# A Mamba-2 block with a SwiGLU feed-forward: the inverse roots of its norm loaded in four pieces, and its hand-written order renewed

## The chip, the cores and the metric

The kernel runs on one core of a Trainium2 chip. Times are microseconds of device time of that core; a comparison takes the median of the runs. TensorE (PE) multiplies matrices, VectorE (DVE) and ScalarE (ACT) do elementwise work and empty PSUM, GpSimd (POOL) does a little, and SyncE (SP) issues nearly all transfers. Each of them works through its own queue of instructions in order and waits on semaphores for the others.

## The reference

Two stages follow each other. The first is a state-space recurrence for 4 sequences with 8 heads, 768 tokens, 32 values and 16 states per head, worked out in chunks:

```python
L = np.exp(cum[:, :, :, None] - cum[:, :, None, :]) * causal
M = np.einsum('bhin,bhjn->bhij', Cc, Bc) * L
y = np.einsum('bhij,bhjd->bhid', M, xc) + inter      # inter: C times the state, decayed
state = decay_full * state + sum(B x, decayed)
```

Its output, as 3072 tokens of 256 values, goes through a norm and a feed-forward with 1536 hidden values:

```python
rms = np.sqrt(np.mean(x * x, axis=-1, keepdims=True) + 1e-06)
xn = x / rms * rms_g
g, val = xn @ w_gate, xn @ w_val
out = (g / (1 + np.exp(-g)) * val) @ w_out
```

The weights and the gain of the norm arrive in 64-bit floating point.

## The kernel before

The tokens are taken in 6 blocks of 512. Values lie with the features on the partitions: y, the squares and the normed input xn are tiles of 128 partitions by 2 x 512 tokens. Block 0 is computed while the weights arrive and are converted to fp32 (`fetch` loads a piece, `pow`, `man` and `wt` convert it on ACT and DVE). From tile 3 of block 0 on, each product with a weight matrix uses a scheme with 7 products in place of 8.

Every step of the kernel has a name, and one long string of about 1,550 names, written out by hand, gives the order in which the steps are issued. A name such as `2:P.5.3` is block 2, step P, arguments 5 and 3; a number behind a slash names a PSUM slot. Each step puts its instructions and its DMAs on the queues of the engines that it uses, so the string fixes the order on every queue. The semaphores follow from the tiles. The steps that are spoken of below:

- `P.k.j` (`product_gv`, L909): product k of 7 for hidden tile j, into one of two PSUM tiles "gate" or "val". `take.k.j` (L915, ACT) copies a partial result p out. `C.c.j` (L921, DVE) adds up c. `silu` (L930, ACT) and `hid` (L934, DVE) make the hidden values h. In block 0, `gate.f` (L825), `early.f.s` (L835) and `norm.f` (L846) do the same for the first tiles without the scheme.
- `s`, `s3`, `s2`, `s4` (L965 to L975, DVE) make combinations of h. `O.k.j` (L999) is product k of 7 with w_out, `Otake` (L1015) and `Oadd` (L1023, L1026) add them up into ob, `out.a` (L1031) and `quarter` (L1036) store. `o.f` (L941) is w_out in block 0.
- `bc.p`, `x.p` (L121, L128) load B, C and x of a pair of chunks; `turn` (L505) transposes B and C on TensorE; `T` (L516) and `Tt` (L1107) copy the result out; `dT` (L530) loads decays dT from rowe in DRAM, and `Td` (L536) multiplies by them. `g`, `gg` (L562) are the products C times B, `L`, `L1` (L601, L607) multiply them by the decays L, `y` (L699) makes the output and starts the additions to the states of the next pairs (L627), `S` (L641, L651) the states. `spread` (L461), `sub`, `ex` prepare L. `yt` (L758 or L763) and `sq` (L747, L749) take y and its squares out of PSUM. `row`, `rowout`, `rowe` (L1074 to L1088) write rows of sums and decays to DRAM. `cw.j` (L879) combines weights.

The norm of blocks 1 to 5 goes through DRAM. `ms` (L777) sums the squares on TensorE: for each of 4 groups of 128 tokens it writes 32 partitions that all hold the same 128 sums. `rs` (L786, L787, ACT) takes the inverse root of this 128 x 128 tile and stores it in DRAM as roots, 4 groups x 32 equal copies x 128 tokens (L790, 64 KB). `rb` (`spread_roots`, L792 to L795) loads them as a tile r of 128 partitions by 512 tokens, 256 KB: each partition reads copy 0 of the 4 groups, 2 KB in all. `xn` (`norm_apply`, L802) multiplies y by the gain and by r, `tx` (L886) makes differences of xn, and then the P products of the next block can start.

Of the kernel before, what the change touches and what calls it, by code (L numbers as in the profile page):

```python
# [20 lines left out]
def kernel(  # L21
# [33 lines left out]
    nc = tc.nc  # L55

    P = 128
    NB, NH, S, D = x.shape
# [5 lines left out]
    T = NB * S  # L64
# [3 lines left out]
    NT = TB // P  # L68
# [104 lines left out]
    parts = {}  # L173
# [31 lines left out]
    warm = const.tile([P, 256], BF16, name="warm")  # L205
    gcol = const.tile([P, 2], FP32, name="gcol")
# [29 lines left out]
    mid = mids[:, 0]  # L236
# [555 lines left out]
    def spread_roots(blk):  # L792
        ps["r", blk] = r = nrm.tile([P, TB], FP32, tag="sq2", name="r", bufs=1)
        nc.sync.dma_start(out=r.rearrange("p (t m) -> p t m", t=NT),
                          in_=roots[blk][:, 0].partition_broadcast(P))  # L795
# [367 lines left out]
    def of_chunk(n, fn):  # L1163
# [28 lines left out]
        0:warm 0:a 0:set 0:bc.0 0:bc.1 0:x.0 0:x.1 0:ident 0:fetch.0 0:ones 0:zeros 0:fetch.1 0:mean  # L1192
        0:head 0:upto 0:never 0:after 0:mid 0:upto2 0:gcol 0:mids 0:ident16 0:whole16 0:idle.7
        0:mask.0.0/1 0:whole 0:hmask 0:tmask 0:part 0:part2 0:sel 0:mask.1.1/0 0:fetch.5 0:after2
        0:aT 0:la0 0:kinks 0:mask.0.1/2 0:log4.0.4 0:r.0 0:parts.0 0:eps 0:log 0:d 0:dx 0:c*2 0:cx
        0:log4.4.2 0:log4.6.2 0:scale.0 0:bc.2 0:turn.0.1 0:T.0.1 0:Tt.0.0.1 0:Tt.0.1.1 0:sums.0.1
        0:exp.0.1 0:turn.0.0 0:Tt.0.1.0 0:T.0.0 0:Tt.0.0.0 0:sums.0.0 0:exp.0.0 0:fetch.2 0:turn.1.1
        0:T.1.1 0:Tt.1.0.1 0:Tt.1.1.1 0:scale.1 0:cc 0:g.0.1/2 0:L.0.1 0:turn.1.0 0:Tt.1.1.0
        0:Tt.1.0.0 0:T.1.0 0:sums.1.1 0:exp.1.1 0:A.0 0:S.0 0:A.1 0:S.1 0:man.0 0:g.0.0/1 0:L.0.0
        0:pow.0 0:wt.0 0:man.5 0:pow.1 0:never16 0:last.1 0:Tl.1 0:mask.1.0/2 0:sums.1.0 0:exp.1.0  # L1200
        0:g.1.0/0 0:L.1.0 0:scale.2 0:last.0 0:Tl.0 0:fetch.4 0:fetch.3 0:x.4 0:middles 0:man.1
        0:g.1.1/1 0:L.1.1 0:fetch.6 0:fetch.7 0:pow.5 0:wt.5 0:y.0/2 0:sq.0 0:pow.3 0:row.1
        0:rowout.1 0:rowe.1 0:yt.0 0:ydone.0 0:fetch.12 0:y.1/0 0:r.1 0:row.0 0:man.2 0:fetch.9
        0:fetch.8 0:wt.1 0:early.0.0/1 0:parts.1 0:man.6 0:mask.3/2 0:sums.3 0:pow.2 0:wt.2 0:rowe.0
        0:rowout.0 0:dT.2 1:dT.0 0:sq.1 0:ms.0 0:yt.1 0:ydone.1 0:early.0.1 0:pow.6 0:wt.6
        0:fetch.13 0:man.3 0:exp.3 0:rs.0 0:man.7 0:wt.3 0:turn.2 0:pow.4 0:xn.0 0:mask.2/0 0:sums.2
        0:exp.2 0:early.1.0/2 0:early.1.1 0:man.4 0:wt.4 0:gate.2/0 0:x.2 0:norm.0 0:norm.1 0:T.2
        0:Tt.2.0 0:Tt.2.1 0:Td.2 0:dT.3 0:gg.2/1 1:table 0:silu.0 0:hid.0 0:gate.3/2 0:tx.0 0:man.8
        0:pow.7 0:wt.7 0:L1.2.3 0:L1.2.2 0:man.9 0:silu.2 0:hid.2 0:L.2.0 0:pow.9 0:wt.9 0:A.2 0:S.2
        0:pow.8 0:wt.8 0:silu.3 0:hid.3 0:fetch.11 0:man.11 0:pow.11 0:gate.4/0 0:silu.4 0:hid.4  # L1210
        0:bc.3 0:scale.3 0:fetch.10 0:pow.10 0:man.10 0:cw.3 0:gate.5/1 0:silu.5 0:hid.5 0:x.3
        0:y.2/2 0:pow.12 0:S.3 0:yt.2 0:sq.2 0:ydone.2 0:switch.0 0:P.1.3 0:take.1.3 0:wt.10 0:wt.11
        0:fetch.14 0:switch.1 0:P.2.3 0:man.12 0:turn.3 0:T.3 0:Tt.3.1 0:Tt.3.0 0:Td.3 0:bc.5
        0:P.6.3 0:take.6.3 0:man.13 0:x.5 0:pow.14 0:P.1.4 0:gg.3/2 0:L1.3.2 0:L.3.0 0:L1.3.3 0:bc.4
        0:scale.4 0:P.7.3 0:scale.5 0:y.3/2 0:silu.1 0:C.11.3 0:take.7.3 0:P.5.3 0:P.4.3 0:P.2.4
        0:wt.12 0:pow.13 1:dT.1 0:fetch.18 1:S.0 1:S.1 0:sq.3 0:yt.3 0:ydone.3 0:C.22.3 0:silug.22.3
        0:P.3.3 0:take.1.4 0:silug.21.3 0:ms.1 0:silug.11.3 0:tok 0:fetch.16 0:tokout 0:cw.4 0:P.6.4
        0:C.11.4 0:P.5.4 0:silug.11.4 0:take.6.4 0:P.7.4 1:turn.1 0:wt.13 0:take.7.4 0:C.12.3
        0:silug.12.3 0:P.2.5 0:pow.16 0:man.14 0:hidg.22.3 0:hidg.21.3 0:P.1.5 0:hidg.11.3 0:wt.14
        0:take.1.5 0:o.0/2 1:bc.1 0:hidg.12.3 0:C.22.4 0:P.3.4 0:silug.22.4 0:fetch.15 0:pow.15  # L1220
        0:cw.5 0:P.6.5 0:hid.1 0:o.1 0:C.11.5 0:take.6.5 0:silug.11.5 0:man.15 0:fetch.17 0:fetch.19
        0:P.4.4 0:spread.10 0:C.12.4 0:pow.17 0:silug.12.4 0:silug.21.4 0:wt.15 0:man.17 0:P.5.5
        0:P.7.5 0:take.7.5 0:man.16 0:wt.16 0:pow.18 0:o.2 0:o.3 0:o.4 0:o.5 0:hidg.11.5 0:P.4.5
        0:cw.1 0:C.22.5 0:silug.22.5 1:two.0 0:spread.9 0:exps 0:wt.17 0:spread.8 0:man.18 0:wt.18
        0:rs.1 1:turn.0 0:hidg.11.4 0:hidg.21.4 0:hidg.22.4 1:T.0 1:Tt.0.0 0:silug.21.5 0:hidg.12.4
        0:P.3.5 0:C.12.5 0:man.19 0:pow.19 0:wt.19 0:hidg.21.5 0:silug.12.5 0:hidg.12.5 0:spread.11
        0:sub.11 0:ex.11 0:table.0 0:sub.8 0:o.6 0:o.7 0:o.8 0:o.9 0:o.10 1:T.1 1:Tt.1.0 0:rb.1
        0:xn.1 1:P.1.1 1:take.1.1 1:P.1.0 1:take.1.0 1:P.2.1 1:P.2.0 0:tx.1 1:P.6.1 1:take.6.1
        0:ex.8 0:hidg.22.5 0:o.11 1:P.7.1 0:sub.9 0:ex.9 1:take.7.1 1:bc.0 0:cw.0 1:P.6.0 2:bc.1
        1:C.11.1 1:P.5.1 0:sub.10 0:ex.10 1:x.0 1:cw.2 1:P.4.1 1:take.6.0 1:P.7.0 2:spread.2  # L1230
        1:C.11.0 1:P.5.0 0:table.1 1:C.22.1 1:P.3.1 1:silu.21.1 1:hid.21.1 1:P.1.2 1:C.12.1
        1:silu.11.1 1:hid.11.1 1:silu.22.1 1:hid.22.1 1:take.7.0 1:C.22.0 1:P.4.0 1:take.1.2
        1:silu.11.0 1:hid.11.0 1:silu.21.0 1:hid.21.0 1:silu.12.1 1:hid.12.1 1:two.4 1:P.2.2 1:P.6.2
        1:take.6.2 1:silu.22.0 1:hid.22.0 1:P.1.3 1:take.1.3 1:P.3.0 1:C.12.0 1:s.1 1:P.7.2
        1:take.7.2 1:P.6.3 1:C.11.2 1:take.6.3 1:silu.11.2 1:two.2 1:P.2.3 1:C.11.3 1:P.4.2
        1:silu.21.2 1:P.5.2 1:C.22.2 1:silu.22.2 1:hid.11.2 1:hid.21.2 1:hid.22.2 1:P.7.3 1:take.7.3
        1:P.5.3 1:C.22.3 0:put.0 0:put.1 0:put.3 1:P.3.2 1:C.12.2 1:Tt.0.1 1:Td.0 1:s3.1 1:P.4.3
        1:silu.21.3 1:hid.21.3 1:silu.11.3 1:hid.11.3 1:silu.12.2 1:hid.12.2 1:P.1.4 1:take.1.4
        1:P.3.3 1:C.12.3 1:silu.12.3 1:hid.12.3 0:put.2 1:Tt.1.1 1:Td.1 1:scale2.1 1:silu.22.3
        1:hid.22.3 1:s.3 1:P.1.5 1:take.1.5 1:P.2.5 1:C.11.5 1:silu.12.0 1:hid.12.0 1:P.6.4  # L1240
        1:take.6.4 1:P.2.4 1:C.11.4 1:silu.11.5 1:hid.11.5 1:P.6.5 1:take.6.5 1:P.7.4 1:take.7.4 1:g
        1:L 1:L1.2 1:P.7.5 1:take.7.5 1:L1.3 1:P.5.4 1:C.22.4 1:P.4.4 1:silu.21.4 1:scale2.0 1:P.5.5
        1:C.22.5 1:silu.22.5 1:hid.22.5 1:silu.11.4 1:hid.11.4 1:hid.21.4 1:y.0 1:P.3.4 1:C.12.4
        2:S.0 1:P.4.5 1:silu.21.5 1:hid.21.5 1:s.2 1:P.3.5 1:C.12.5 1:silu.22.4 1:hid.22.4 1:s.0
        1:O.2.0 1:O.2.1 1:silu.12.4 1:hid.12.4 1:s.4 1:s3.4 1:O.1.0 1:O.1.1 1:silu.12.5 1:hid.12.5
        1:O.4.0 1:O.1.2 1:O.1.3 1:x.1 1:y.1 2:S.1 1:sq 1:spread.0 1:yt 1:O.1.4 1:O.1.5 1:Otake.1
        1:s.5 1:exps 1:spread.2 1:s3.3 2:dT.0 1:O.4.1 1:O.4.2 1:O.5.0 1:s2.0 1:O.5.1 1:s2.1 1:O.5.2
        1:s2.2 1:O.5.3 1:O.5.4 1:s2.4 1:s2.3 1:O.5.5 1:s2.5 1:s3.2 1:s3.0 1:sub.2 1:ms 1:rs 1:O.6.0
        1:s4.0 1:O.6.1 1:O.6.2 1:s4.1 1:O.6.3 1:O.6.4 1:O.6.5 1:Otake.6 1:s4.3 1:s4.4 2:turn.0 2:T.0
        2:Tt.0.1 1:rb 1:s4.5 1:s4.2 1:s3.5 2:dT.1 2:turn.1 2:T.1 2:Tt.1.0 2:Tt.1.1 2:Tt.0.0 2:Td.0  # L1250
        1:sub.0 1:ex.0 1:O.2.2 1:O.7.0 1:O.7.1 1:O.7.2 1:O.7.3 1:O.7.4 1:O.7.5 1:Otake.7 1:Oadd.22
        2:scale2.1 1:O.4.3 1:O.4.4 1:O.4.5 1:Oadd.21 1:O.2.3 1:O.2.4 1:O.2.5 1:O.3.0 1:O.3.1 1:xn
        2:P.1.1 2:take.1.1 2:P.1.0 2:take.1.0 1:tx 1:ex.2 1:spread.1 1:sub.1 1:ex.1 1:O.3.2 1:O.3.3
        1:O.3.4 1:O.3.5 1:Oadd.12 1:spread.3 1:sub.3 1:ex.3 2:P.6.0 2:take.6.0 2:x.0 2:P.6.1
        2:take.6.1 1:Oadd.11 2:P.2.1 2:C.11.1 2:silu.11.1 2:P.2.0 2:C.11.0 2:silu.11.0 2:hid.11.0
        2:P.7.0 2:take.7.0 2:P.7.1 2:take.7.1 2:P.5.0 2:C.22.0 2:silu.22.0 2:P.5.1 2:C.22.1
        2:silu.22.1 2:P.4.0 2:silu.21.0 2:hid.21.0 2:P.4.1 2:silu.21.1 2:hid.21.1 2:hid.11.1 2:P.3.1
        2:C.12.1 2:silu.12.1 2:P.3.0 2:C.12.0 2:silu.12.0 2:hid.12.0 2:Td.1 2:P.1.2 2:take.1.2
# [130 lines left out]
```

## Time and profile before

| | us |
|---|---|
| median of three runs | 407.25 |
| lowest and highest of them | 405.87 and 407.42 |
| the profiled execution | 406.08 |
| its span in the profile | 404.3 |
| TensorE busy in it | 395.5 |
| VectorE, ScalarE, GpSimd busy | 296.5, 223.9, 37.6 |

The span is the profile's own time from the first to the last instruction; 1.8 us of the profiled execution lie around it. The profile's line numbers are those of the kernel before. A record of a matmul is longer than the interval at which matmuls follow each other when the queue is full: for L909 the record has 0.38 us and the interval is 0.22, for L999 0.28 and 0.11. So the busy share of TensorE says that something was in its pipeline, and where it stood still is read from the gaps. A transfer has two records, the issue on the SP queue and the landing, and the DMA table gives the time between.

The stretches of the span: state space and weights to about 72 us, the rest of block 0 and its w_out to about 98 us, and then one block of the feed-forward after the other, each with the state space of a later block beside it. ms of blocks 1 to 5 stands at 66.6, 148.7, 204.2, about 270 and 331.5 us, and r<-roots is issued at 87.00, 151.52, 207.07, 272.62 and 334.30.

### The profile page before, as it was taken

To read this page: it belongs to the slowest core of one execution; us is meant where nothing else is said; L and a number is where in the kernel's file an instruction comes from. 1 tells how busy PE (TensorE), PEld (TensorE's weight loads), DVE (VectorE), ACT (ScalarE), POOL (GpSimd) and SP (SyncE) were. 2 spreads that over 40 slices of the span, in tenths; PEclk is the share of its full clock that TensorE was granted. 3 is DMA by queue.
4 is the path that set the end of the run, shared out by engine and by line. 5 is a ranking of instruction groups with operands and counts; after the bars stand their busy time and mean duration, and the time that the engine had idled before them with its cause. 6 is when DMAs were issued, how large, how long until landed. Compare 5 with 4: busy or idle time off the path is not lost.

```text
span 404.3 us, 9559 instructions
## 1 busy us (share of the span) xinstructions
PE 395.5 (98%) x3881; PEld 338.6 (84%) x3881; DVE 296.5 (73%) x686; ACT 223.9 (55%) x456; POOL 37.6 (9%) x57
## 2 busy tenths in 40 slices
PE   8989999999999998999999999999999999999997
PEld 5656467888888898988899888899988899988896
DVE  6999999987687885567786566877657666475772
ACT  3989986967756343744552654372674461445410
POOL 2210000002300011400011300011400010000000
PEclk9999999999999999999999999999999999999999
DMA  9988968427001126600414210303000003100001
GB/s 112 203 248 222 219 89 230 129 44 93 27 0 54 29 73 103 67 0 4 106 51 115 46 34 0 69 8 92 1 2 2 2 2 87 52 0 2 0 2 52
DMA packets 92355, 26.99 MB, mean 67 GB/s; under 512 B 77048, under 2 KB 86136, under 8 KB 92312
## 3 DMA queue, kind: packets, MB, share of 16 engines
q1 hardware_dynamic: 88152, 26.13, 30.8%
q10 hardware_dynamic: 4160, 0.26, 0.8%
q8 instruction: 30, 0.49, 0.5%
q14 instruction: 13, 0.11, 0.1%
HBM read 22.64 MB, written 3.74 MB: 65 GB/s over the span
## 4 chain that ended last, share of the span: by engine, by line
PE 85%; DVE 6%; DMA 4%; ACT 2%; issue 1%; SPq 1%; DVEq 0%; ACTq 0%
PE gate L909 28%; PE val L909 21%; PE o L999 17%; PE o L941 5%; PE gate L825 3%; PE y L699 3%; DMA r<-roots 2%; DMA dT<-rowe 2%; PE gate L835 1%; PE g L562 1%; PE y L627 1%; PE e L426 1%; DVE m L195 1%; DVE wgv L201 1%; DVE xn L802 1%
## 5 line engine op out<-in xcount | busy, mean ns | idle before, releaser
L921 DVE TENSOR_TENSOR c<-val,p 128x512 f32<-128x512 f32 x99 | 67.8, 689 | 35.1 <-PE val L909 30.9
L915 ACT COPY p<-gate 128x512 f32<-128x512 f32 x99 | 57.4, 581 | 51.9 <-PE gate L909 47.6
L909 PE MATMUL gate<-tx,sw 128*128 128x256 f32 x264 | 65.6, 382 | 0.0
L930 ACT ACTIVATE c<-c 128x256 f32<-128x256 f32 x99 | 39.7, 415 | 44.2 <-DVE c L921 44.1
L909 PEld LDWEIGHTS gate<-tx,sw 128*128 128x128 f32 x264 | 49.3, 190 | 7.4 <-ACT p L915 0.5
L934 DVE TENSOR_TENSOR h<-c 128x256 f32<-128x256 f32 x99 | 40.4, 420 | 11.4 <-ACT c L930 10.9
L909 PE MATMUL gate<-xn,wgv 128*128 128x256 f32 x132 | 33.4, 383 | 1.4 <-DVE xn L802 1.3
L909 PE MATMUL val<-xn,sw 128*128 128x256 f32 x132 | 33.7, 381 | 0.8 <-DVE c L921 0.8
L909 PE MATMUL val<-tx,sw 128*128 128x256 f32 x132 | 33.4, 381 | 0.0
L909 PE MATMUL val<-xn,wgv 128*128 128x256 f32 x132 | 33.2, 380 | 0.0
L909 PE MATMUL gate<-tx,wgv 128*128 128x256 f32 x132 | 32.8, 380 | 0.0
L475 POOL TENSOR_SCALAR_AFFINE_SELECT L<-L 64x512 f32<-64x512 f32 x32 | 23.6, 738 | 92.1 <-ACT L L473 90.6
L999 PE MATMUL o<-wo,h 128*128 128x128 f32 x240 | 30.3, 277 | 0.0
L999 PEld LDWEIGHTS o<-wo,h 128*128 128x128 f32 x240 | 28.7, 192 | 0.9 <-issue 0.4
L909 PEld LDWEIGHTS gate<-xn,wgv 128*128 128x128 f32 x132 | 24.3, 190 | 5.3 <-issue 1.6
L999 PE MATMUL o<-two,s 128*128 128x128 f32 x240 | 28.7, 275 | 0.0
L909 PEld LDWEIGHTS val<-xn,sw 128*128 128x128 f32 x132 | 24.7, 190 | 4.5 <-DVE c L921 1.2
L999 PE MATMUL o<-two,h 128*128 128x128 f32 x240 | 28.4, 275 | 0.0
L999 PEld LDWEIGHTS o<-two,s 128*128 128x128 f32 x240 | 27.8, 192 | 0.3 <-issue 0.2
L909 PEld LDWEIGHTS val<-tx,sw 128*128 128x128 f32 x132 | 24.8, 190 | 3.4
L909 PEld LDWEIGHTS gate<-tx,wgv 128*128 128x128 f32 x132 | 24.8, 190 | 3.3
L999 PEld LDWEIGHTS o<-two,h 128*128 128x128 f32 x240 | 27.6, 192 | 0.0
(188 smaller groups left out, 612.3 us busy)
## 6 DMA issues: line engine op xcount, KB each, us to landing
L<-rowd SPq DMA_DIRECT2D x32, 128.0 KB, 5.9
xr<-in_x_dram SPq DMA_DIRECT2D x24, 128.0 KB, 4.3
wr<-in_moe_w_out_dram SPq DMA_DIRECT2D x6, 512.0 KB
wr<-in_moe_w_val_dram SPq DMA_DIRECT2D x5, 512.0 KB, 7.1
wr<-in_moe_w_gate_dram SPq DMA_DIRECT2D x5, 512.0 KB, 6.6
out_dram<-ob SPq DMA_DIRECT2D x9, 256.0 KB, 2.6
br<-in_B_dram SPq DMA_DIRECT2D x22, 64.0 KB, 4.2
cr<-in_C_dram SPq DMA_DIRECT2D x22, 64.0 KB, 3.3
```

Source lines behind the costliest of these rows:

```text
L195: nc.vector.scalar_tensor_tensor(out=f, in0=lo.bitcast(U32), scalar=2.0 ** -32, in1=m, op0=ALU.mult, op1=ALU.add)
L201: nc.vector.scalar_tensor_tensor(out=dst, in0=f, scalar=2.0 ** -20, in1=e, op0=ALU.mult, op1=ALU.mult)
L475: nc.gpsimd.affine_select(out=L[r], in_=L[r], pattern=[[0, NH], [1, HC]], compare_op=ALU.is_ge, fill=0.0, base=0, channel_multiplier=-1)
L699: nc.tensor.matmul(out=y[2 * k + u][rows, (2 * n + i) * HC:(2 * n + i + 1) * HC], start=(k, u, rows.start) not in opened, stop=True, skip_ ...
L825: nc.tensor.matmul(out=gv[:, k], lhsT=w[:, t, fs], rhs=xns[0][:, t], start=(t == 0), stop=(t == 1))
L909: nc.tensor.matmul(out=dst[:, half[w]], lhsT=lhsT, rhs=rhs, start=(k in (1, 2, 5) and w == 0), stop=True, skip_group_check=True)
L915: nc.scalar.copy(out=t, in_=Xs[j])
L921: nc.vector.tensor_tensor(out=t, in0=Zs[j], in1=a, op=ALU.add)
L930: nc.scalar.activation(out=u, in_=src[:, half[0]], func=AF.Silu)
L934: nc.vector.tensor_tensor(out=hidden_tile(blk, j)[:, c // 10 - 1, c % 10 - 1], in0=u, in1=src[:, half[1]], op=ALU.mult)
L941: nc.tensor.matmul(out=o, lhsT=hs_[blk, f // 2][:, f % 2, k // 2, (k % 2) * P:(k % 2 + 1) * P], rhs=wo[:, f], start=opens, stop=(f == NF - ...
L999: nc.tensor.matmul(out=o[t] if apart else o[:, t * P:(t + 1) * P], lhsT=lhsT[:, t], rhs=rhs, start=(k in (1, 2, 4, 5) and j == 0 and (apar ...
```

## The change

It has two parts. First, the load of r is cut in four, by 32 partitions each, and each partition of such a group reads another one of the 32 stored copies:

```diff
     def spread_roots(blk):
         ps["r", blk] = r = nrm.tile([P, TB], FP32, tag="sq2", name="r", bufs=1)
-        nc.sync.dma_start(out=r.rearrange("p (t m) -> p t m", t=NT),
-                          in_=roots[blk][:, 0].partition_broadcast(P))
+        for k in range(P // 32):
+            nc.sync.dma_start(
+                out=r[32 * k:32 * k + 32].rearrange("p (t m) -> p t m", t=NT),
+                in_=roots[blk].rearrange("t q m -> q t m"))
```

Second, the same 1,548 steps stand in a new order. In the first 130 or so, the steps move past each other mostly between engines, and the order on each engine hardly changes: on ACT one logarithm (`log4.4.2`) moves ahead of two exponentials, and TensorE's order is the same up to the 35th of its steps. From there on, near 28 us of the profile, every queue has a new order. Two stretches of the string, cut to the steps that matter here:

```diff
-        0:rowout.0 0:dT.2 1:dT.0 0:sq.1 0:ms.0 0:yt.1 0:ydone.1 0:early.0.1 0:pow.6 0:wt.6
-        0:fetch.13 0:man.3
-        0:exp.3 0:rs.0 0:man.7 0:wt.3 0:turn.2 0:pow.4 0:xn.0 0:mask.2/0 0:sums.2
-        0:exp.2 0:early.1.0/2 0:early.1.1 0:man.4 0:wt.4 0:gate.2/0 0:x.2 0:norm.0 0:norm.1 0:T.2
...
-        0:P.1.4 0:gg.3/2 0:L1.3.2 0:L.3.0 0:L1.3.3 0:bc.4
-        0:scale.4 0:P.7.3 0:scale.5 0:y.3/2 0:silu.1 0:C.11.3 0:take.7.3 0:P.5.3 0:P.4.3 0:P.2.4
-        0:wt.12 0:pow.13 1:dT.1 0:fetch.18 1:S.0 1:S.1 0:sq.3 0:yt.3 0:ydone.3 0:C.22.3 0:silug.22.3
-        0:P.3.3 0:take.1.4 0:silug.21.3 0:ms.1 0:silug.11.3 0:tok 0:fetch.16 0:tokout 0:cw.4 0:P.6.4
-        0:C.11.4 0:P.5.4
+        0:sq.1 0:ms.0 0:yt.1 0:ydone.1 0:early.0.1 0:man.3 0:wt.3 0:mask.2/2 0:sums.2 0:pow.6 0:fetch.8
+        0:wt.6 0:man.4 0:x.2 0:exp.3 0:early.1.0/1 0:rs.0 0:norm.0 0:xn.0 0:pow.4 0:wt.4 0:fetch.10
+        0:man.7 0:dT.3 0:turn.2 0:early.1.1 0:norm.1 0:rowout.0 0:exp.2 1:table 0:man.9 0:silu.0
+        0:hid.0 0:gate.2/0 0:T.2 0:Tt.2.0 0:Tt.2.1 0:Td.2 0:pow.7 0:fetch.14 0:wt.7 0:tx.0 0:gg.2/1
...
+        0:gg.3/2 0:L1.3.3 0:L.3.0 0:L1.3.2 0:bc.4 0:scale.4 0:P.2.4 0:P.7.3 0:bc.5 0:scale.5 0:x.5
+        0:y.3/2 0:wt.12 0:take.7.3 0:C.11.3 0:P.5.3 0:silug.11.3 0:pow.13 1:S.0 0:fetch.18 0:P.4.3
+        1:dT.0 0:C.22.3 0:P.3.3 0:take.1.4 0:silug.22.3 0:cw.4 0:P.6.4 0:silu.1 0:silug.21.3 0:C.11.4
+        0:silug.11.4 0:take.6.4 0:P.5.4 0:P.7.4 1:S.1 0:sq.3 0:yt.3 0:ydone.3 1:turn.1 0:tok
```

And the edge from block 1 to block 2, from the sum of squares to the first product, in full:

```diff
-        1:ms 1:rs 1:O.6.0
-        1:s4.0 1:O.6.1 1:O.6.2 1:s4.1 1:O.6.3 1:O.6.4 1:O.6.5 1:Otake.6 1:s4.3 1:s4.4 2:turn.0 2:T.0
-        2:Tt.0.1 1:rb 1:s4.5 1:s4.2 1:s3.5 2:dT.1 2:turn.1 2:T.1 2:Tt.1.0 2:Tt.1.1 2:Tt.0.0 2:Td.0
-        1:sub.0 1:ex.0 1:O.2.2 1:O.7.0 1:O.7.1 1:O.7.2 1:O.7.3 1:O.7.4 1:O.7.5 1:Otake.7 1:Oadd.22
-        2:scale2.1 1:O.4.3 1:O.4.4 1:O.4.5 1:Oadd.21 1:O.2.3 1:O.2.4 1:O.2.5 1:O.3.0 1:O.3.1 1:xn
-        2:P.1.1
+        1:ms 1:rs 1:O.5.4 1:O.5.5 1:s2.5 1:s2.4 1:rb 1:ex.2 2:turn.0 2:T.0 2:Tt.0.1 2:Tt.0.0
+        1:O.6.0 1:s4.0 1:O.6.1 1:s4.1 1:O.6.2 1:s4.2 1:O.6.3 1:s4.3 2:turn.1 2:T.1 2:Tt.1.0 1:s3.4
+        1:s3.5 1:O.6.4 1:s4.4 1:O.6.5 1:Otake.6 1:s4.5 1:O.4.2 1:O.4.3 1:O.7.0 1:O.7.1 1:O.7.2
+        1:O.7.3 1:O.7.4 1:O.7.5 1:O.2.3 1:O.4.4 1:O.4.5 1:sub.0 1:ex.0 1:O.2.4 1:O.2.5 1:Otake.7
+        1:Oadd.22 1:O.3.0 1:Oadd.21 1:O.3.1 1:O.3.2 1:xn 2:P.1.0
```

On the other edges the old and new order hold, between `ms` and the first P step of the next block: block 2, 36 and 35 O steps with 2 turns each; block 3, 33 O and 1 turn, then 34 O and 2 turns; block 4, 26 and 28 O steps; block 0, 12 P and 11 o steps, then 8 P and 11 o steps. Of the two dT transfers of block 3, `3:dT.1` and `3:dT.0` stood behind `2:rb` before (the first 18 steps behind it, the second later); now `3:dT.1` stands ahead of `2:ms`, and `3:dT.0` far behind `2:rb`, with `3:Td.0`, which uses it, as the next step. At the end, `5:out.1` moves behind `5:quarter.0.0`.

## The prediction

> **What bounds the kernel now.** First the head of the page: span, busy shares, and the chain that ended last by line.
>
> ```profile
> span 404.3 us, 9559 instructions
> PE 395.5 (98%) x3881; PEld 338.6 (84%) x3881; DVE 296.5 (73%) x686; ACT 223.9 (55%) x456; POOL 37.6 (9%) x57
> ...
> PE gate L909 28%; PE val L909 21%; PE o L999 17%; PE o L941 5%; PE gate L825 3%; PE y L699 3%; DMA r<-roots 2%; DMA dT<-rowe 2%; PE gate L835 1%; PE g L562 1%; PE y L627 1%; PE e L426 1%; DVE m L195 1%; DVE wgv L201 1%; DVE xn L802 1%
> ```
>
> TensorE is without a record for only 404.3 - 395.5 = 8.8 us, at full granted clock. The change leaves every matmul in place, so it can win only from those 8.8 us and from the refill of the pipeline after each gap. The 2% (8.4 us) of r<-roots in the chain are not 8.4 us of standstill: TensorE multiplies beside the load. So I went on to TensorE's gaps.
>
> Of the 8.8 us, 1.1 lie ahead of the first matmul and 2.9 behind the last (401.4 to 404.3: an add, a store, the closing). The other 4.8 are twelve gaps. Those in the waits view of TensorE, 21 to 72 us:
>
> ```profile
> PE y L677 <- DVE L L601: 0.8, 1, 0.8
> PE val L909 <- DVE c L921: 0.8, 1, 0.8
> PE r_ps L1074 <- ACT e_sb L1087: 0.4, 1, 0.4
> PE y L699 <- DVE L L601: 0.4, 1, 0.4
> PE tp L505 <- ACT sq L747: 0.3, 1, 0.3
> ```
>
> After 72 us only two are left, 1.27 at 160.82 and 0.17 at 222.74. The first is the roots. The timeline (start, length, what; in brackets the idle time before):
>
> ```profile
> 151.52 0.37 SPq L794 DMA_DIRECT2D r<-roots  x1
> ...
> 159.92 1.42 DVE L802 SCALAR_TENSOR_TENSOR xn<-yt,gcol,r 128x512 f32<-128x512 f32 x2 [2.15 <-DMA r<-roots]
> ...
> 160.82 1.96 PE L909 MATMUL gate<-xn,wgv 128*128 128x256 f32 x8 [1.27 <-DVE xn L802]
> ```
>
> The load issues at 151.52 and lands at 159.90, VectorE scales xn, and TensorE starts 1.27 us after it ran dry. In the other four blocks the load is hidden: VectorE waits for r in three blocks, 5.7 us in all, TensorE in one.
>
> **Part 1, the load in four.** Removed: five loads of 256 KB. Added: twenty of 64 KB. The DMA table (KB each, us to landing):
>
> ```profile
> br<-in_B_dram SPq DMA_DIRECT2D x22, 64.0 KB, 4.2
> cr<-in_C_dram SPq DMA_DIRECT2D x22, 64.0 KB, 3.3
> ...
> r<-roots SPq DMA_DIRECT2D x5, 256.0 KB, 8.2
> ...
> roots<-r SPq DMA_DIRECT2D x5, 64.0 KB, 1.5
> ```
>
> 256 KB in 8.2 us is 32 GB/s, where some slices of the page show 250. Before, all 128 partitions read the same 2 KB; after, the 32 partitions of one transfer read 32 different stored copies. The trace has no split load. Low end: the store of those 64 KB, 1.5, behind three more issues at 0.37 (the row at 151.52): 2.6. High end: a rule of the Trainium skill, "DMA: Bandwidth & Descriptors", section "Rules for kernel authors": transfers to disjoint partition groups use the same DMA engines and serialize, so a split is no use. By it the load keeps its 8.4 and adds 1.1 of issues: 9.5. The row speaks against that: at 32 GB/s it isn't the sharing of full engines that limits this load. I take the 64 KB load of C, 3.3, issued back to back as these will be: 1.1 + 3.3 = 4.4, nearer the low end.
>
> Its worth at 160.82: from the end of ms (149.14) to the first gate matmul are 11.7 us: 2.4 to the issue, 8.4 load, 0.9 xn and start. With 4.4 it is 7.7. TensorE's work in between: an O step is four matmuls at 0.111 = 0.444 (16 took 1.78 in the chain), a turn 0.44. Old: 21 O + 2 turns = 10.2, too short by about the gap. New: 24 O + 2 turns = 11.5; the other blocks hold 35 O + 2 turns = 16.4, 34 O + 2 turns = 16.0, 28 O = 12.4, and over 26 in block 0. All exceed 7.7. The VectorE steps ahead of xn (s4, sub, two Oadd) are fed by O steps that stand several O earlier, so xn queues behind nothing late. Gain 1.27, plus 0.16 of refill (in a filled L909 stretch matmuls start every 0.22 with records of 0.38; a gap loses the overlap): **-1.4**. By the rule the path is 2.4 + 9.5 + 0.9 = 12.8 against 11.5 and 12.4: gaps of 1.3 and 0.4, that is +0.4 in place of -1.4.
>
> The three extra issues, 1.1 us a block, stand ahead of L, dT, x and B/C loads on SP's queue. SP waits 92.9 us in all just for r before its stores, and the transfers behind the roots get the DMA engines sooner. Cost 0; without that cover, up to 1.1 at a later wait.
>
> **Part 2, dT at 222.74.** One row of the chain:
>
> ```profile
> 208.19 8.09 DMA dT<-rowe
> ```
>
> dT was issued behind r<-roots (207.07) and landed when that was through; VectorE waited 2.16 for it, and xn and tx came late. In the new order one dT of this block stands ahead of the roots, the other far behind with its user. 0.17 + 0.16: **-0.3**.
>
> **Part 3, the order from 28 us.** (a) The copy r_sb (0.21 to the next start) no longer stands ahead of yt.1, for which the matmul at 29.16 waited 0.14: with refill **-0.3**. To 57.9 us I laid ACT's and DVE's rows in the new order: rs.0 still ends near 30.9, norm.0 and xn.0 by 34.5, wt.4 by 35.2, while gate.2 can't start before 36.1 by TensorE's own work. The SiLU table load now stands ahead of T.2, whose copies end at 37.1 instead of 35.0; gg.2 needs them at 39.6. Cost 0, cover 2.5; gone, it would cost the excess.
>
> (b) At 59.99 y.3 waited 0.36 for L. Now P.2.4 (0.86) also stands ahead of it: closed. (c) P.3.3 at 65.57 waited 0.76 for c, queued behind S.0 and S.1. S.1 now comes after:
>
> ```profile
> 63.66 0.42 DVE L641 TENSOR_TENSOR A<-y,tmask 128x128 f32<-128x128 f32 x2
> 64.00 0.92 DVE L651 SCALAR_TENSOR_TENSOR S<-S,fcol,A 128x64 f32<-128x64 f32 x3
> ```
>
> These two rows, 1.2 us, leave the path, but y.3 itself runs 0.36 later: c ends at 64.7, P.3.3 starts 0.8 earlier than 65.57, with the same matmuls done. (d) A new wait: P.5.4 follows P.6.4 directly, where ms.1 and tok (0.9) stood between before. C.11.4 is queued behind cw.4's four operations (1.7) and ends near 67.1, TensorE is there at 66.6: +0.5. (b) to (d): **-0.3**.
>
> The 1.8 us of gaps ahead of 25 us stay: the order there is almost the same (one logarithm moves into an idle ACT, under 0.1). The end: out.1 is issued after quarter.0.0, about 0.9 us later than before; its packets ran 0.8 us, and the last quarter's start only at 402.6. Cost 0; if they met, up to 0.8. Steps from 72 us on are otherwise reordered under a TensorE without gaps: that can only cost. I value it at 0 and keep up to 1.5 for the range.
>
> Sum: -1.4 - 0.3 - 0.3 - 0.3 = -2.3, span 404.3 to 402.0, the profiled execution's 406.08 to 403.8. The median of the three runs, 407.25, is 1.2 above the profiled one: 405.0.
>
> **Rivals.** (A) As worked out, 405.0, own range 404.0 to 405.8: 0.53. (B) The reorder trades old waits for new: two or three like (d), 1.5 us, somewhere in the 330 us whose order is new. For it: VectorE is busy 73%, over 90% to 80 us. Against it: from 72 us on the old order had two gaps. 407.25 - 2.3 + 1.5 = 406.5: 0.28. (C) The split doesn't do what it says, by the rule: -2.3 + 1.8 = 406.8: 0.09. (D) More is won, because most of the early waits (0.8 and 0.4) and the tail shrink too: another 1.2, 403.8: 0.05. (E) Slower: each of the four transfers waits for the one before, 4 x 3.3 = 13.2, the path 16.5 against 11.5, 16.4, 16.0, 12.4: gaps of 5.0, 0.1, 0.5 and 4.1 = 9.7 on top of the sum: 414.7. It decides from a load of 8.2 us (11.5 - 3.3). Against it: B and C loads are issued about 0.6 apart and still land in 3.3 to 4.2. 0.05.
>
> **How the numbers follow.** 0.5% is 2.0 us, about what a measurement of this kernel can tell from no change; it lies at 405.2. Faster: most of A and all of D, 0.55. Same: the rest of A, B, C: 0.39. Slower: E and a bad B, 0.06. The three runs alone lie 1.5 us apart. Range 402.8 (D with a low run) to 406.9 (B and C in).
>
> **What would show it.** Right: the last r<-roots piece lands under 5 us after the first issue; no DVE wait for r; no TensorE gap before xn at any block; gaps near 59.99 gone and one of about 0.5 at P.5.4. Wrong: pieces landing 3 us apart (E) or at 9 us (C), or new waits of L909 on c, p or h after 72 us (B).

## The result and the profile after

| | us |
|---|---|
| before, median of 9 runs | 407.28 (405.87 to 407.82) |
| after, median of 9 runs | 404.67 (403.26 to 405.70) |
| ratio | 0.994, 95% interval 0.9924 to 0.9956 |
| profiled execution after, and its span | 404.06 and 402.1 |

The change saves 2.6 us, 0.6%; 405.0 was forecast. First the page of the changed kernel: span, busy times, chain by line (numbers from L795 on are two higher than before).

```profile
span 402.1 us, 9591 instructions
PE 394.8 (98%) x3881; PEld 338.9 (84%) x3881; DVE 297.9 (74%) x686; ACT 224.5 (56%) x456; POOL 37.6 (9%) x57
...
PE gate L911 28%; PE o L1001 24%; PE val L911 21%; PE o L943 5%; PE gate L827 4%; PE y L699 3%; PE gate L837 2%; PE g L562 2%; SPq L121 1%; DMA wr<-in_moe_w_val_dram 1%; PE tp L505 1%; SPq L128 1%; DMA br<-in_B_dram 1%; PE y L627 1%; SPq L160 1%; PE ms L777 0%
```

TensorE is busy about as long as before (394.8 against 395.5), and r<-roots and dT<-rowe have left the lines of the chain shown here. From the waits view of TensorE (total, times, longest):

```profile
PE r_ps L1076 <- ACT e_sb L1089: 0.9, 1, 0.9
PE y L677 <- DVE L L601: 0.8, 1, 0.8
PE val L911 <- DVE c L923: 0.5, 1, 0.5
```

The wait of 0.4 for L at y.3 is gone, the one for c is 0.5 in place of 0.8, and the one for e_sb is 0.9 in place of 0.4, which was not foreseen. After 68 us the timeline shows no gap of TensorE. The timeline at the edge from block 1 to 2, and the DMA table:

```profile
150.39 1.76 SPq L795 DMA_DIRECT2D r<-roots  x4
157.93 1.41 DVE L804 SCALAR_TENSOR_TENSOR xn<-yt,gcol,r 128x512 f32<-128x512 f32 x2
```

```profile
r<-roots SPq DMA_DIRECT2D x20, 64.0 KB, 2.3
```

No idle time stands before xn: r was there. Each piece lands 2.3 after its issue, so the last about 3.7 after the first. To place the gain I compared the times at which TensorE had done equal amounts of its work. The table gives the differences to the kernel before that arose in each stretch, with two experiments of the next section beside the changed kernel:

| stretch (us of before) | predicted | after | order alone | load alone |
|---|---|---|---|---|
| to 36, (a) | -0.3 | +0.09 | -0.36 | -0.03 |
| 36 to 75, (b) to (d) | -0.3 | -0.28 | -0.29 | 0.00 |
| to 168, edge of block 2 | -1.4 | -1.53 | -1.52 | -1.53 |
| to 236, edge of block 3 | -0.3 | -0.52 | -0.38 | -0.41 |
| the rest | 0 | -0.04 | -0.05 | -0.01 |
| sum | -2.3 | -2.28 | -2.60 | -1.98 |

### The profile page after: what moved, and what is told of

Same layout as the page of the kernel before. It is cut to its first block, busy times and chain, and to the rows that moved or that the text cites. A ratio compares the mean times of both kernels' runs of the same rounds, so it can differ in the third digit from the quotient of the medians.

```text
span 402.1 us, 9591 instructions
## 1 busy us (share of the span) xinstructions
PE 394.8 (98%) x3881; PEld 338.9 (84%) x3881; DVE 297.9 (74%) x686; ACT 224.5 (56%) x456; POOL 37.6 (9%) x57
## 4 chain that ended last, share of the span: by engine, by line
PE 91%; SPq 3%; DMA 2%; DVE 1%; ACT 1%; issue 0%
PE gate L911 28%; PE o L1001 24%; PE val L911 21%; PE o L943 5%; PE gate L827 4%; PE y L699 3%; PE gate L837 2%; PE g L562 2%; SPq L121 1%; DMA wr<-in_moe_w_val_dram 1%; PE tp L505 1%; SPq L128 1%; DMA br<-in_B_dram 1%; PE y L627 1%; SPq L160 1%; PE ms L777 0%
## 5 line engine op out<-in xcount | busy, mean ns | idle before, releaser
L911 PEld LDWEIGHTS val<-xn,wgv 128*128 128x128 f32 x132 | 24.8, 190 | 3.5 <-issue 0.2
```

The source lines that it names most:

```text
L911: nc.tensor.matmul(out=dst[:, half[w]], lhsT=lhsT, rhs=rhs, start=(k in (1, 2, 5) and w == 0), stop=True, skip_group_check=True)
```

## The experiments

**Which half pays.** Two kernels undo one half each. The first has the new order and the old load:

```diff
-        for k in range(P // 32):
-            nc.sync.dma_start(
-                out=r[32 * k:32 * k + 32].rearrange("p (t m) -> p t m", t=NT),
-                in_=roots[blk].rearrange("t q m -> q t m"))
+        nc.sync.dma_start(out=r.rearrange("p (t m) -> p t m", t=NT),
+                          in_=roots[blk][:, 0].partition_broadcast(P))
```

> The new order with the old single load of r. In its trace the time between ms and the first gate matmul of block 2 is 2.4 + 8.4 + 0.9 = 11.7 us against 11.5 us of O steps and turns in the new order. Theory (the order gives the load more cover, so either half of the change closes the 1.27 gap of TensorE ahead of block 2): a gap of 0.2 to 0.4 is left there, the other edges stay closed, dT of block 3 no longer waits, and the time is 0.2 to 0.6 above the changed kernel, near 405.2. Rival 1 (only the faster load pays): the gap stays above 1, the time is near 406.3. Rival 2 (the new order itself costs): slower than the kernel before. The gap near 25.0 us that grew from 0.39 to 0.89 should be here as well if the order makes it, and back near 0.4 if it was the chance of one run.

Measured: 404.87 (the kernel before, measured beside it: 406.92), ratio 0.9944 (0.9926 to 0.9961). The same edge in its timeline:

```profile
149.93 0.37 SPq L794 DMA_DIRECT2D r<-roots  x1
158.16 1.42 DVE L802 SCALAR_TENSOR_TENSOR xn<-yt,gcol,r 128x512 f32<-128x512 f32 x2 [0.60 <-DMA r<-roots]
159.16 1.89 PE L909 MATMUL gate<-xn,wgv 128*128 128x256 f32 x8
```

The load still takes 8.2, VectorE waits 0.60 for it, and TensorE starts its gate product with no gap in front: the longer row of O steps just covers the 11.6 us from the end of ms to that product. The gap of 0.2 to 0.4 that I expected is not there, and both rivals fall. The gap at r_ps is 0.25 here, in the same order that had 0.89.

The second has the old order and the new load, the diff of the change's first part alone.

> The old order with the load of r in four, each partition from its own copy. Path from ms to the first gate matmul of block 2: 2.4 + 3.7 + 0.9 = 7.0 us (the load by its length in the changed kernel) against 10.2 us of O steps and turns. Theory: the gap of 1.27 ahead of block 2 is gone, and as dT is queued behind r, the 0.17 ahead of block 3 too: 1.5 to 1.9 less than before, near 405.5; the gaps ahead of 72 us stay as before (0.39 near 24.5, 0.14 near 29.2, 0.36 near 60.0, 0.76 near 65.6). Rival 1 (the new order pays): the time stays within 0.5 of before. Rival 2 (three more issues ahead of the other loads on the SP queue cost, and the new order makes up for it): new waits of TensorE or VectorE on L, dT or x, and less than 1.0 gained.

Measured: 404.79, ratio 0.9954 (0.9936 to 0.9972). Its timeline and its waits:

```profile
151.48 1.76 SPq L795 DMA_DIRECT2D r<-roots  x4
157.64 1.41 DVE L804 SCALAR_TENSOR_TENSOR xn<-yt,gcol,r 128x512 f32<-128x512 f32 x2
159.33 1.89 PE L911 MATMUL gate<-xn,wgv 128*128 128x256 f32 x8
```

```profile
PE val L911 <- DVE c L923: 0.8, 1, 0.8
PE gate L837 <- DVE yt L758: 0.4, 1, 0.4
PE y L699 <- DVE L L601: 0.4, 1, 0.4
```

The gaps at both block edges are closed, and the early waits for c, yt and L of the old order are there. No new wait for L, dT or x appears, so the three more issues cost nothing. Together with the first kernel: each half closes both edges by itself. The halves do not add up. In the old order the load is worth 2.0; in the new order it is worth nothing that shows (ratio 0.9944 without it, 0.994 and 0.9942 in two measurements with it).

**What makes the load fast.** Three loads in the old order, one run each; as runs of one kernel differ by up to 2.4 us, the traces decide here and not the times. Four pieces as in the change, but all of copy 0:

```diff
-                in_=roots[blk].rearrange("t q m -> q t m"))
+                in_=roots[blk][:, 0].partition_broadcast(32))
```

> The old order, the load of r in four by 32 partitions, but every partition reads copy 0: the split without own copies. Theory (128 partitions reading the same 2 KB is what makes the load slow): the four pieces together still take 7 to 9 us from the first issue, VectorE waits for r, and TensorE keeps a gap of about 1.3 ahead of block 2; if the issues hold it up as well, up to 2.4. Rival (smaller transfers or four at once are what helps): the last piece lands 3 to 4.5 us after the first issue, no gap ahead of block 2, as in the load alone.

Measured: 406.20 (before: 407.36). Its waits on VectorE and on TensorE:

```profile
DVE xn L804 <- DMA r<-roots: 5.7, 3, 2.9
```

```profile
PE gate L911 <- DVE xn L804: 1.4, 1, 1.4
```

VectorE waits 5.7 us in three blocks, exactly as before, so the split by itself brings nothing. What the load sees shows in the DMA view from 151.5 to 160.5 us, moved GB/s in 40 slices of 0.225 us, first of this kernel, then of the load alone:

```profile
GB/s 0 0 0 0 20 41 50 36 48 50 36 48 46 43 43 46 36 36 27 50 57 23 34 32 50 43 48 46 14 71 148 239 216 246 323 342 307 319 313 244
```

```profile
GB/s 0 0 0 0 114 162 66 207 96 182 82 194 64 0 127 182 205 209 250 182 127 246 128 100 182 200 128 182 250 142 144 191 201 212 194 171 100 42 22 14
```

Some 5.4 us lie flat near 45 GB/s while all partitions read one copy. In the trace's packets that is 512 reads of 512 bytes, one per 13 to 14 ns, though half of them took 27 ns or less; with own copies the same reads came one per 4 ns.

Then one load, with the copies stored as runs of 2 KB by four stores: each partition from its own copy (partition p reads copy p/4), and all from copy 0.

```diff
+            for k in range(NT):
+                nc.sync.dma_start(out=roots[blk][:, k], in_=r[32 * k:32 * k + 32])
...
+        nc.sync.dma_start(out=r, in_=roots[blk].rearrange("q t m -> q (t m)").unsqueeze(1)
+                          .to_broadcast([32, P // 32, TB]))
```

> The old order, one load of 256 KB, but the 32 copies are stored each as one run of 2 KB (by four stores in place of one, some 1 us more ahead of the load), and partition p reads copy p/4. Theory: 32 places in place of one, so 64 readings... four readers each, and the load lands 2 to 4 us after its issue; no VectorE wait for r longer than 1 and no TensorE gap ahead of block 2. Rival (the split helps): it keeps about 8 us and, with the later stores, the gap grows to 2.

> As the one before (four stores, runs of 2 KB, one load), but all 128 partitions read copy 0. It sets the length of the runs apart from the number of places read. Theory: slow as in the kernel before, 6 to 9 us to landing, gap ahead of block 2 of 1.5 to 2.3. Rival (what was slow is reading in runs of 512 bytes): 2 to 4 us, as with own copies.

Measured: 404.14 and 403.82, no VectorE wait for r in either. The line of the DMA table, first with own copies, then of copy 0:

```profile
r<-roots SPq DMA_DIRECT2D x5, 256.0 KB, 2.8
```

```profile
r<-roots SPq DMA_DIRECT2D x5, 256.0 KB, 3.5
```

My theory held for the first and fell for the second: one place read by all 128 partitions is not slow if it is read in 128 long runs. What was slow is the two together, one copy and runs of 512 bytes. In block 5, where nothing else of this size was under way, the 128 reads of 2 KB from one copy came one per 15 ns, but from own copies also only one per 11 ns. One reading fits all these loads: one copy gives about one read per 13 ns, whatever its length, and the old load needed 512 of them. For runs of 2 KB it is not shown, as 15 and 11 lie close.

To see from how many copies on this is over, three loads cut in four by the groups of tokens, in place of the single load. They read from copies 0 and 1 (shown), from eight, and from copies 0 and 16:

```diff
+        for t in range(NT):
+            nc.sync.dma_start(out=r[:, t * P:(t + 1) * P],
+                              in_=roots[blk][t, 0:2].unsqueeze(1)
+                              .to_broadcast([2, P // 2, P]))
```

> The old order; the load of r in four by the 4 groups of 128 tokens, runs of 512 bytes, 64 partitions reading copy 0 and 64 copy 1. Theory, as it stands after the three loads before (reads of one place are served one after the other, so what counts is the number of reads of each place; 128 reads of each of 4 places took 6.6 us in the old load, 128 reads of one place of 2 KB about 2): 64 reads of each of 8 places, half of 6.6 and the 1.3 of issues and some 1.5 of start, the last landing 5 to 6 us after the first issue. Rival (neighbouring copies count as one place, or the number of 512-byte reads is the cost): 8 to 9 us as with copy 0 alone.

> As the one before with 8 copies, 16 partitions reading each. Theory: 0.8 us of reads of one place, less than the four issues take, so the last landing 3.3 to 4.2 us after the first issue, as with 32 copies (3.7). Rival: 8 to 9 us.

> As the load from two copies, but copies 0 and 16, 8 KB apart in place of 512 bytes. Neighbouring copies 0 and 1 served one read of 512 bytes per 12 to 13 ns, as copy 0 alone did, eight copies one per 4.7 ns at most. Theory (neighbours share what serves them one read at a time; copies far apart don't): half of 6.4 us, or 6 to 7 ns for each read, the last of the 512 reads ends 4.5 to 5.5 us after the first issue. Rival (what counts is how many copies there are, not where they lie): 12 to 13 ns again, the last ends at 7.8 to 8.8.

Measured, from the first issue to the end of the 512th read: 7.8 to 8.8 us, 3.8 to 4.1, and 8.3 to 9.0. The times were 408.87, 405.69 and 413.34 (the kernel before: 406.45 beside the first two, 405.92 beside the third), so both kernels that load from two copies are slower than the kernel before. With two copies TensorE waits 1.5 and 2.6 for xn ahead of block 2 and 1.6 for ob later; with eight it has no gap there. By my wording the rival would hold for two copies. The packets point elsewhere: with two copies two or three reads are in flight most of the time, most of them of 25 to 29 ns; with eight copies it is eight or nine in the middle of a piece. That fits loads dealt to two and to eight DMA engines, and 27 / 2 = 13.5 ns is all that the slow ones show. The Trainium skill has the rule, "DMA: Bandwidth & Descriptors", section "Why a DMA increments its semaphore by 16 and not by 1": the number of engines is the largest up to 16 that divides the slowest dimension of both sides. Here that dimension is 2 or 8, and the reads in flight agree; the trace does not name the engines. So the two slow loads say nothing of places; that eight copies are enough stands. The old load is no such case: at the edge of block 2 it had up to 17 reads in flight at once, the loads from two copies 4 at most.

**The first 40 us.** The gap of 0.89 at r_ps: e_sb stands on ACT behind pow.3, which waited for a weight piece. ACT before, after, and in a repeat of the changed kernel (the last column is the wait):

```profile
22.68 0.53 ACT L182 ACTIVATE e<-wr,kinks 128x256 int16<-128x256 int16 x1 [1.17 <-DMA wr<-in_moe_w_val_dram]
```

```profile
23.17 0.53 ACT L182 ACTIVATE e<-wr,kinks 128x256 int16<-128x256 int16 x1 [1.66 <-DMA wr<-in_moe_w_val_dram]
```

```profile
23.55 0.53 ACT L182 ACTIVATE e<-wr,kinks 128x256 int16<-128x256 int16 x1 [2.04 <-DMA wr<-in_moe_w_val_dram]
```

Three edits of the changed kernel's order (`rowe.1` is e_sb; the second builds on the first, the third on the second), and the repeat:

```diff
-  0:row.1 0:pow.3 0:rowout.1 0:yt.0 0:ydone.0 0:rowe.1
+  0:row.1 0:rowout.1 0:yt.0 0:ydone.0 0:rowe.1 0:pow.3
...
-  0:man.1 0:pow.5 0:L.1.1 ... 0:row.0 0:man.2 0:fetch.9 0:wt.1
+  0:pow.5 0:L.1.1 0:man.1 ... 0:row.0 0:wt.1 0:man.2 0:fetch.9
...
-  0:man.6 0:mask.3/1 0:sums.3 0:pow.2 0:wt.2 0:rowe.0 0:dT.2 0:sq.1 0:ms.0 0:yt.1 0:ydone.1
+  0:sq.1 0:yt.1 0:ydone.1 0:man.6 0:mask.3/1 0:sums.3 0:pow.2 0:wt.2 0:rowe.0 0:dT.2 0:ms.0
```

> The changed kernel with one step moved: the logarithm and exponential of a weight piece (pow.3, three operations of ACT, 1.6 us, waiting for its DMA) stands behind the copy e_sb (rowe.1) instead of ahead of it. Theory (the gap of TensorE near 25.0, 0.89 us, is e_sb queued behind an ACT step that waits for a weight): the gap closes to under 0.2, and up to 0.8 is gained, near 404.0; the next to be late is the weight piece 1 on VectorE. Rival 1 (the weight piece is then late by as much, and a gap opens near 35 us at gate.2 or earlier): no change within 0.3. Rival 2: another step ahead of e_sb on ACT sets it, the gap stays above 0.6.

> As the one before, and on VectorE two mantissa steps of weight pieces (man.1, 0.8 us, ahead of L.1.1; man.2 ahead of wt.1) moved behind the steps for which TensorE waits. Theory (the gap near 22.2, 0.79 us, is y waiting for L, queued behind man.1): both gaps shrink, 0.5 to 1.1 gained against the changed kernel, near 403.8, bounded by xn.0 and weight piece 4 near 35 us. Rival 1 (the moved work comes late at the next user): no change within 0.3, and new gaps between 25 and 37 us as long as those closed. Rival 2 (ACT's L ends last, not VectorE's queue): the gap at 22.2 stays.

> The kernel with rows and mantissa moved, and the squares and the taking out of y.1 (sq.1 on ACT and GpSimd, yt.1 on VectorE) moved ahead of the weight steps pow.2 and man.6. Theory (ms waited 0.98 for sq on GpSimd because sq.1 stood behind two pow steps on ACT; the weights themselves come early enough): that gap goes, TensorE's gaps between 20 and 36 us fall from 1.7 to about 1.0 or less, and the time is 0.4 to 1.0 under the changed kernel in the same call. Rival (the loads of the weights set this stretch, and every move only shifts the gap): gaps of 1.3 to 1.8 again, at the gate products near 34 us, and no change within 0.3.

> The changed kernel once more, beside the one before on the same chip. Theory (its gap of 0.89 near 25 us was the landing of one weight piece in one execution, not the order): the gap here lies between 0.1 and 0.6, and the time is 404.0 to 405.0. Rival (the order makes it): 0.8 to 0.9 again.

Measured: the first 403.83, ratio 0.9924 (0.9909 to 0.9939); the second 404.26, 0.9943 (0.9920 to 0.9965); then, beside a kernel before of 406.45, the third 403.85, 0.9934 (0.9914 to 0.9953), and the changed kernel 404.23, 0.9942 (0.9920 to 0.9965). TensorE's gaps between 20 and 36 us:

| kernel | at y (L) | r_ps (e_sb) | new ones | sum |
|---|---|---|---|---|
| changed | 0.79 | 0.89 | | 1.68 |
| changed, repeat | 0.78 | 1.28 | | 2.06 |
| first edit | 0.79 | 0 | 0.69 ms (sq), 0.61 gate (yt) | 2.09 |
| second edit | 0.13 | 0.33 | 0.29 e (row), 0.98 ms (sq) | 1.74 |
| third edit | 0.12 | 0.32 | 0.74 e (row) | 1.18 |

The repeat falls outside both of its expectations: the gap at r_ps is 1.28. Over all executions it is 0.25, 0.89 and 1.28 in the new order, and 0.39, 0.09, 0.34, 0, 0.36, 1.08, 0 and 0 in the old: it follows the landing of one weight piece in that execution, and the ranges overlap. In their profiles the first and second edit moved the gap to the next user (rival 1). Only the third clearly shortened the sum; its median lies 0.4 under that of the changed kernel beside it (six runs each, 403.56 to 404.04 against 403.81 to 404.71), 0.1%. That is too small to call sure. By its ratio the first edit (0.9924) lies even lower than the third (0.9934), though its gaps are longer, and the intervals of all these versions overlap: which of them is fastest is not shown.

## Why the prediction was right, and where it wasn't

- **The edge of block 2, -1.4:** -1.53. The mechanism held, but the entry stood under part 1 alone. The order alone closes the gap too: my own numbers had 11.7 of path against 11.5 of cover for the old load in the new order, a gap of 0.2 at most, and I didn't draw the conclusion that the load would then be worth almost nothing.
- **The load, 4.4 us:** about 3.7, with 1.35 to the fourth issue in place of 1.1 and 2.3 to land in place of 3.3. The rule on disjoint partitions is right about the split: four pieces of one copy gain nothing. What it doesn't speak of, reading other copies, is what made the load fast; I gave the gain to both without telling them apart.
- **dT, -0.3:** -0.52 in that stretch, and -0.38 and -0.41 by either half: the old order with a fast load frees dT behind it, the new order puts dT ahead of it. VectorE's wait of 2.16 for dT is gone in both halves and is still 1.97 with four pieces of copy 0. The term was too small: in the load alone, the time gained between 222 and 223 us, around the gap of 0.17, is 0.43.
- **(a), -0.3:** +0.09 after, but -0.36 with the order alone. The wait at 29.16 is gone in the three profiles of the new order and stood at 0.12 to 0.64 in every run of the old one; in the first edit of the new order it came back with 0.61. In the profile after, the late weight piece at 25.0 took it back.
- **(b) to (d), -0.3:** -0.28. Inside, c ended at 64.9, near the 64.7 worked out, but P.3.3 still waited 0.45 for it, so TensorE reached P.5.4 at 66.97 and not at 66.6, and the new wait (d) was 0.07 in place of 0.5.
- **0 from 72 us on, and at the end:** no gap after 68 us, the rest -0.04; rival B did not occur. The last matmul ends 2.28 earlier, the span 2.2. That the sum, -2.28, meets the -2.3 so closely is luck in part: (a) fell 0.4 short, and the two block edges gave 0.35 more than forecast.
- **Rivals C and E:** the last piece lands at 3.7, neither at 9 nor at 13.

What stays open is what holds reads of one copy at 13 ns each, the memory or something on the way; how few copies would do, as the loads from two were slow for another reason; and whether the third edit's lead is real.

## What to carry to other kernels

A late transfer at a block edge can be cured by a faster transfer or by more work ahead of its user; cost each with the other one in place before adding them up. When many partitions need the same values, count the reads that go to one copy: fewer, longer runs or more stored copies both help, cutting the transfer doesn't. And a gap in an early stretch that waits for a load needs a second profile before it is put down to an order of steps.

## What the runs showed of the hardware

512 reads of 512 bytes from one 2 KB copy came one per 13 to 14 ns, with three to six of them in flight on average; from 32 copies they came one per 4 ns. 128 reads of 2 KB came one per 15 ns from one copy and one per 11 ns from 32 (block 5). Loads whose slowest dimension was 2 had two or three reads in flight and took some 8 us for 256 KB.

Executions of one kernel lie up to 2.4 us apart (the changed one 403.26 to 405.70). The two profiles of the first and the second edit lie 1.7 apart (404.03 and 405.77), and this falls ahead of 13 us: with TensorE's order the same up to there, the first g product began at 10.61 and at 12.54. Early on, the same matmuls ran at half their later speed for a shorter or longer time. The same product in the first edit and in the second edit (the next one began 0.32 and 0.64 after it):

```profile
6.08 0.49 PE L379 MATMUL d_ps<-la,upto 128*128 128x192 f32 x2
```

```profile
7.09 0.85 PE L379 MATMUL d_ps<-la,upto 128*128 128x192 f32 x2
```

The clock records of the traces agree: the full clock is granted from 3.9 us in the first edit, 5.2 in the changed kernel, 5.5 in the kernel before, 9.6 in the second edit and 9.9 in the load from copies 0 and 16. The Trainium skill, "TensorE: Matmul & The Clock Gate", section "Part 1: The HAM clock gate (the "warmup" mystery)", says that the window that raises the clock, 3.4 us long, runs free of the kernel's start, and gives 0.5 us either way for the point of change. Here that point lay between 3.9 and 9.9 us, a spread of more than one such window; what moved it so far is not shown. The 1.9 us between the two g products are nearly as large as what this change gains, which is why medians of several runs were needed.

The clock can also fall again. In the load from copies 0 and 16, TensorE's gap of 2.61 ahead of block 2 was followed by 3.4 us at half the clock:

```profile
163.66 3.56 PE L911 MATMUL gate<-xn,wgv 128*128 128x256 f32 x8 [2.61 <-DVE xn L804]
```

The same eight matmuls took 1.96 us in the kernel before, behind a gap of 1.27. So the late load cost more there than the gap itself. After the gaps of 1.5 and 1.6 in the load from copies 0 and 1 the clock did not fall.
